# Attention and a tanh-shrink MLP on one core: the last twelve attention steps take their scores in pairs, with a down product between, and two stores change queue

## The chip, the cores and the metric

One core of a Trainium2 chip runs the whole program. The metric is the device time of one execution in microseconds (us). The profiler's times count from the first instruction of the execution that was profiled.

## The reference

For each of 4 batches and 8 heads (768 tokens, 64 dims), queries and keys are assigned to one of 16 clusters; a query attends only to keys of its own cluster. The attention output feeds an MLP with the activation h - tanh(h).

```python
q_assign = np.argmax(np.einsum('bhsd,hcd->bhsc', q_n, c_n), axis=-1)
k_assign = np.argmax(np.einsum('bhsd,hcd->bhsc', k_n, c_n), axis=-1)
mask = q_assign[:, :, :, None] == k_assign[:, :, None, :]
scores = np.where(mask, scale * (q @ k.transpose(0, 1, 3, 2)), -1e9)
attn = softmax(scores);  x = attn @ v          # (4, 8, 768, 64) -> (3072, 512)
h = x @ w_in                                    # w_in 512 x 2048
out = (h - np.tanh(h)) @ w_out                  # w_out 2048 x 512
```

## The kernel before

The attention runs as 96 **steps** (`steps`): per batch four pairs of heads, per pair two halves of the queries, per half three steps of two key chunks each. A step on TensorE is one score group (`sc`, line 544, eight matmuls in the trace: 64 rows of the array for each of two heads), then on ScalarE the exponential (line 566), on VectorE the **select** (line 576, four instructions: weight kept where the cluster codes agree), on GpSimd the running sum of the weights (`sum`, lines 588 and 592), and on TensorE the value product (`av`, line 601). The scores lie in two PSUM buffers, one for each key chunk; a group can start on a buffer when the select has read it.

The MLP of the batch before fills the time between. It is done by Strassen's scheme: **up products** (`pu`) and, for each of seven factor products and each block of 128 tokens, a **down product** (`pd`, line 1301: 32 matmuls in the trace, 16 in the program, each in two passes) whose result VectorE adds to running sums (`w_in`, `c`, line 1317). The list `fill` holds these items with weights, and each step takes as many as its share of the weight (`spent`, `whole`). Items and the other work of a step (`todo`) are written out by hand, so each engine runs exactly the order that the program lists.

TensorE works in two forms here: the scores use 64 rows by 128 columns (a trace row shows `64*128`), av, pu and pd use 128 rows by 64 columns (`128*64`). A product can also be written in the scores' form (`rows_`, `three_in_rows`): then a down product needs two of the three PSUM buffers `ps_f` and each result is added in two instructions. `runs(at)` names the steps at which the scores of the next three steps are issued together with such products between; the last twelve steps (84 to 95) are not among them: there each step has one score group, one av and mostly one pd.

Around it: `check_done` and `check_on` read inputs again (`again`, two buffers): `check_done` reduces two loaded tiles on VectorE (lines 1776 and 1781), `check_on` issues two new loads on SyncE's queue (SP). For the row sums, SP carries `list`, `each`, `back` and `den` through DRAM: VectorE's reciprocal of `each` (line 714), then the store `back` (line 716), then four loads `den` (line 737). `set_aside` stores factors of one block, and a sum of them that VectorE makes in `u` (line 1266), for later. `divide` takes reciprocals of `den` in three parts (line 764), and GpSimd adds them up (`inverses`, line 768). After step 95 the rest is the tail: `pu` of the last batch and then its down products (`pp`).

Of the kernel before, what the change touches and what calls it, by code (L numbers as in the profile page):

```python
# [58 lines left out]
def kernel(  # L59
# [120 lines left out]
    def fast():  # L180
# [677 lines left out]
        behind = []  # L858
# [346 lines left out]
        def strassen_items(b: int):  # L1205
# [33 lines left out]
            def weight(i: int):  # L1239

                return 4.55 if aside_ else 3.4
# [10 lines left out]

            def set_aside(which: int):

                d = [i for i in range(len(ASIDE)) if ASIDE[i][0] == b]
                for i in d:
# [12 lines left out]
                    behind.append(lambda total_=total_, i=i: nc.sync.dma_start(  # L1269
# [8 lines left out]
            def down_product(k_: int, j: int, between, rows_=False):  # L1278
# [66 lines left out]
                if j < 2:  # L1345
                    if k_ == 2:
                        behind.append(lambda: lower_aside(6, j))
                    elif k_ == 4:
                        behind.append(lambda: lower_aside(3, j))
                    if (k_, j) in SET_ASIDE:  # L1350
                        behind.append(lambda: set_aside(SET_ASIDE[k_, j]))
# [142 lines left out]
            def group(at: int):  # L1494
# [64 lines left out]
                if final:  # L1559
                    add(m, m, u0)  # L1560
                    nc.sync.dma_start(row(0, 1, 0)[:, 0:HC], quarters[:, 0])
                    nc.sync.dma_start(row(0, 1, 1)[:, HC:HM], quarters[:, 3])
# [284 lines left out]
        def runs(at: int):  # L1847

            return 4 * HALF < at < 7 * HALF - 1 and at % NS == NS - 1 and at % (2 * HALF) < 2 * HALF - 1

        fill, whole, spent, since, over = [], 0.0, 0.0, 0, 1
        for at, (n, half, s) in enumerate(steps):
# [21 lines left out]
            if run:  # L1874
                coming = now + fill
                for _ in range(NS - 1):
# [5 lines left out]
                while len(now) < first_ones + 1:  # L1882
# [3 lines left out]
            elif runs(at + 1):  # L1886
                ups_left = sum(len(it) == 4 for it in fill)
                if ups_left < 3 * (NS - 1):
# [17 lines left out]
            if run:  # L1906
                take(n, half)
                if half == 1 and joined(n):
                    total_both(n)
# [17 lines left out]
                begin(steps[at + NS])  # L1927
                while off:
                    off.pop(0)()
                begun |= set(steps[at + 1 : at + NS + 1])  # L1930
                selected |= set(steps[at + 1 : at + NS + 1])
                held = [
                    lambda i=i, to=steps[at + NS]: select(*to[:2], 2 * to[2] + i) for i in range(2)
# [67 lines left out]
            if following and not run:  # L2001

                if half == 1 and s == NS - 1 and joined(n):
                    todo.insert(len(todo) - 1, lambda n=n: total_both(n))
# [9 lines left out]
            if not run and not runs(at + 1):  # L2014
                todo += behind
                behind.clear()
# [28 lines left out]
            if "raw" in late_pools:  # L2045
                if not run and not runs(at + 1) and at != 7 * HALF:
# [46 lines left out]
        for it in late + behind:  # L2093
# [240 lines left out]
```

## Time and profile before

| | us |
|---|---|
| three runs | 925.0, 922.12, 924.77 (median 924.77) |
| the profiled execution, its own time | 922.68 |
| its span, first to last instruction | 920.8 |

The mean granted TensorE clock over the span is 0.999 of full speed. Steps 84 to 95 lie between 653 us (score group of step 84) and 751 us; the tail's first up product that needs new differences (`diff`) starts at 759.88 us, and the last stage (`pp`) at 829.6 us.

### The profile page before, as it was taken

The page shows a single profiled execution, that of the slowest core. Times are in us where ns is not written, and L with a number is a line of the kernel's source. Part 1 is how long each engine was busy: PE and PEld are TensorE (multiplying, and loading weights), DVE is VectorE, ACT ScalarE, POOL GpSimd, SP SyncE. Part 2 cuts the span into 40 slices and gives each one's busy share as a digit, 9 for nine tenths or more (in the row PEclk, how much of TensorE's full clock was granted, in tenths as well). Part 3 has the DMA queues.
Part 4 walks back from the last instruction along what each step waited for, and adds up shares of the span by engine and source line. Part 5 has one row for each costly group of instructions (what it writes and reads, how often), then busy time and mean ns, then how long its engine had stood idle before and what let it go on. Part 6 is the DMA issues. An engine that isn't in the chain of part 4 may idle for free.

```text
span 920.8 us, 18740 instructions
## 1 busy us (share of the span) xinstructions
PE 908.1 (99%) x7286; PEld 498.5 (54%) x7286; DVE 692.9 (75%) x1280; ACT 295.2 (32%) x466; POOL 523.6 (57%) x403
## 2 busy tenths in 40 slices
PE   8999999999999999999999999999999999999997
PEld 4434433356653454445666664555455554449997
DVE  7779777887799598667477477767697587867995
ACT  5676653234333233333321121343231311221000
POOL 0236433467878565977765565787776866772000
PEclk9999999999999999999999999999999999999999
DMA  8777583794428985375584746566546745524532
GB/s 168 226 221 180 155 194 105 229 266 141 107 86 224 272 261 141 120 189 175 159 191 151 186 143 169 177 179 161 178 150 205 230 156 155 189 103 151 196 105 85
DMA packets 187439, 158.37 MB, mean 172 GB/s; under 512 B 119200, under 2 KB 161744, under 8 KB 184144
## 3 DMA queue, kind: packets, MB, share of 16 engines
q1 hardware_dynamic: 177696, 134.40, 51.9%
q0 software_dynamic: 6048, 20.98, 6.9%
q10 hardware_dynamic: 3600, 1.74, 0.7%
q8 instruction: 59, 0.97, 0.4%
q14 instruction: 36, 0.29, 0.1%
HBM read 130.33 MB, written 26.75 MB: 171 GB/s over the span
## 4 chain that ended last, share of the span: by engine, by line
PE 92%; DVE 4%; ACT 1%; issue 1%; DMA 1%; POOL 0%; SPq 0%; DVEq 0%; ACTq 0%
PE pu L1021 20%; PE sc L544 15%; PE av L601 14%; PE pd L1301 12%; PE pp L1519 9%; PE o L803 6%; PE pu L1012 5%; PE h L787 5%; PE hd L1152 3%; PE sim L405 1%; DVE e L576 1%; PE den L674 1%; PE den L647 1%; PE den L627 1%; POOL G L1215 0%
## 5 line engine op out<-in xcount | busy, mean ns | idle before, releaser
L592 POOL TENSOR_TENSOR sum<-sum,e 128x768 f32<-128x768 f32 x112 | 206.5, 1844 | 78.7 <-DVE e L576 73.9
L576 DVE SCALAR_TENSOR_TENSOR e<-row,code,sc 128x384 f32<-128x384 bf16 x336 | 184.0, 608 | 56.7 <-ACT sc L566 31.6
L566 ACT ACTIVATE sc<-sc 128x768 f32<-128x768 f32 x168 | 126.4, 793 | 203.0 <-PE sc L544 182.4
L544 PE MATMUL sc<-t,t 64*128 64x384 f32 x768 | 149.1, 505 | 1.6 <-DVE e L576 1.1
L601 PE MATMUL av<-e,vals 128*64 128x384 f32 x768 | 143.4, 495 | 0.0
L1021 PE MATMUL pu<-xT,w_in 128*64 128x384 f32 (+1 forms) x872 | 132.5, 441 | 0.2 <-DVE c L1317 0.2
L1215 POOL TENSOR_TENSOR G<-G,th 128x768 f32<-128x768 f32 (+1 forms) x51 | 88.1, 1745 | 58.1 <-ACT th L1213 58.0
L1301 PE MATMUL pd<-w_in,G 128*64 128x256 f32 (+1 forms) x960 | 108.8, 379 | 0.0
L544 PEld LDWEIGHTS sc<-t,t 64*128 64x128 f32 x768 | 67.8, 186 | 70.5 <-issue 32.7
L1021 PEld LDWEIGHTS pu<-xT,w_in 128*64 128x64 f32 x872 | 61.6, 137 | 62.2 <-issue 50.2
L1301 PEld LDWEIGHTS pd<-w_in,G 128*64 128x64 f32 (+1 forms) x960 | 74.0, 147 | 35.6 <-issue 6.3
L601 PEld LDWEIGHTS av<-e,vals 128*64 128x64 f32 x768 | 49.7, 136 | 77.3 <-issue 73.5
L588 POOL TENSOR_TENSOR sum<-e 128x768 f32<-128x768 f32 x28 | 52.4, 1872 | 60.4 <-DVE e L576 46.4
L1021 PE MATMUL pu<-diff,w_in 128*64 128x384 f32 x416 | 74.1, 488 | 0.5 <-DVE u L1006 0.4
L1213 ACT ACTIVATE th<-G 128x768 f32<-128x768 f32 (+1 forms) x51 | 39.5, 806 | 107.8 <-DVE G L1006 90.9
L803 PE MATMUL o<-w_out,g 128*64 128x512 f32 x256 | 57.4, 593 | 0.0
L1021 PEld LDWEIGHTS pu<-diff,w_in 128*64 128x64 f32 x416 | 29.3, 137 | 37.9 <-issue 31.5
L1006 DVE TENSOR_TENSOR G<-pu,u 128x384 f32<-128x384 f32 x72 | 38.8, 550 | 13.5 <-PE pu L1021 12.1
L1012 PE MATMUL pu<-diff,w_in 64*128 64x384 f32 x160 | 45.8, 482 | 0.0
L1012 PE MATMUL pu<-xT,w_in 64*128 64x384 f32 x152 | 45.1, 482 | 0.0
L787 PE MATMUL h<-xT,w_in 128*64 128x384 f32 x256 | 42.8, 486 | 0.0
L638 ACT COPY xT<-av 128x384 f32<-128x384 f32 x32 | 15.3, 480 | 82.1 <-PE av L601 82.0
(283 smaller groups left out, 1286.0 us busy)
## 6 DMA issues: line engine op xcount, KB each, us to landing
w_in<-up_factors SPq DMA_DIRECT2D x32, 896.0 KB
w_in<-down_factors SPq DMA_DIRECT2D x25, 1024.0 KB
again<-in_moe_w_in_dram SPq DMA_DIRECT2D x32, 256.0 KB
again<-in_moe_w_out_dram SPq DMA_DIRECT2D x32, 256.0 KB
vals<-in_v_dram SPq DMA_DIRECT2D x32, 192.0 KB
raw<-in_moe_w_in_dram POOLq DMA_DIRECT2D x12, 512.0 KB, 4.8
row<-q_codes SPq DMA_DIRECT2D x29, 192.0 KB
raw<-in_moe_w_out_dram POOLq DMA_DIRECT2D x10, 512.0 KB, 4.8
```

The costliest lines, as they stand in the source:

```text
L544: nc.tensor.matmul(sc[i][:, h, 0:TB], lhsT=turned[n, 1][r].rearrange("p a n -> p (a n)")[:, j * P : (j + 1) * P], rhs=turned[n, 0][r, half ...
L566: nc.scalar.activation(out=out, in_=sc[i][:, :, 0:TB], func=ACT.Exp, scale=SCALE)
L576: nc.vector.scalar_tensor_tensor(out=e[:, h].rearrange("p (j n) -> p j n", n=P), in0=rows[n, half][:, h], scalar=(codes[n][:, h, 1, j : j ...
L592: nc.gpsimd.tensor_tensor(out=s, in0=s, in1=pair[i], op=ALU.add)
L601: nc.tensor.matmul(avs[n, half][h * D : h * D + D], lhsT=vals[n][:, h, j], rhs=e[i][:, h], start=(j == 0), stop=(j == NCH - 1),)
L787: nc.tensor.matmul(h[r], lhsT=w_in[i][:, c, o * P : (o + 1) * P][:, r], rhs=xT[c][:, half], start=(c == 0), stop=(c == CD - 1),)
L803: nc.tensor.matmul(acc[sub][r], lhsT=gs[f % HF][:, f // HF, sub * P : (sub + 1) * P][:, r], rhs=w_out[f // FQ][:, f % FQ], start=(f == seq ...
L1012: return nc.tensor.matmul(ps, lhsT=streams[base + i][r, c, k_], rhs=right[c][r], start=start, stop=stop)
L1021: nc.tensor.matmul(ps[r], lhsT=streams[base + i][:, c, k_, r], rhs=right[c], start=(c == 0), stop=(c == CH - 1),)
L1215: nc.gpsimd.tensor_tensor(out=t, in0=t, in1=th, op=ALU.subtract)
L1301: nc.tensor.matmul(out_, lhsT=w, rhs=x, start=(i == 0), stop=(i == HF - 1))
L1519: nc.tensor.matmul(ps[r], lhsT=left[:, i, r], rhs=right[i], start=(i == 0), stop=(i == HQ - 1),)
```

## The change

The steps 84 to 95 get runs of two: `runs` returns 2 at the steps 83, 85, ..., 93. At such a step the program issues the score group of the next step, the selects of it, one chunk of the filling work in the scores' form (three up products at step 83, one down product after), and the score group of the step after that. The weights of the down products of batch 2 become 5.4 for the first twelve and 3.3 for the last two (4.55 for all before). `check_done` and `check_on` now also stand in a step ahead of a run of two, and in the run itself ahead of its selects. The stores of the sums set aside get a list of their own, `stores`. The two first of the four last stores go to ScalarE's queue, where the other two are.

```diff
--- before.py
+++ after.py
@@ -855,7 +855,7 @@
         SET_ASIDE = {
             (0, 0): 1, (0, 1): 5, (1, 0): 2, (1, 1): 4, (2, 0): 7, (3, 0): 6, (5, 0): 3
         }
-        behind = []
+        behind, stores = [], []
         aside = dram.tile([len(ASIDE), 7, P, HF + HQ, P], F32, name="aside", bufs=1)
 
         def up_maker(q: int):
@@ -1238,7 +1238,10 @@
 
             def weight(i: int):
 
-                return 4.55 if aside_ else 3.4
+                if not aside_:
+                    return 3.4
+                i = i // HCH * (HCH - aside_) + i % HCH
+                return 5.4 if i < 12 else 3.3
 
             def lower(j: int, which: int, part: int):
 
@@ -1250,8 +1253,13 @@
                 else:
                     nc.gpsimd.tensor_tensor(out=a12, in0=a12, in1=a11, op=ALU.subtract)
 
+            def store_sums():
+                while stores:
+                    stores.pop(0)()
+
             def set_aside(which: int):
 
+                store_sums()
                 d = [i for i in range(len(ASIDE)) if ASIDE[i][0] == b]
                 for i in d:
                     c = slice(ASIDE[i][1] * P, (ASIDE[i][1] + 1) * P)
@@ -1266,7 +1274,7 @@
                     nc.vector.tensor_tensor(
                         out=total_, in0=t[:, 0:HQ], in1=t[:, HQ:HF], op=ALU.add
                     )
-                    behind.append(lambda total_=total_, i=i: nc.sync.dma_start(
+                    stores.append(lambda total_=total_, i=i: nc.sync.dma_start(
                         aside[i, SLOT[which], :, HF : HF + HQ], total_
                     ))
 
@@ -1342,7 +1350,7 @@
                     lower(j, 6, 1)
                 elif which in (7, 4):
                     lower(j, 3, k_ - 3)
-                if j < 2:
+                if aside_ and j < 2:
                     if k_ == 2:
                         behind.append(lambda: lower_aside(6, j))
                     elif k_ == 4:
@@ -1558,8 +1566,8 @@
                 )
                 if final:
                     add(m, m, u0)
-                    nc.sync.dma_start(row(0, 1, 0)[:, 0:HC], quarters[:, 0])
-                    nc.sync.dma_start(row(0, 1, 1)[:, HC:HM], quarters[:, 3])
+                    nc.scalar.dma_start(row(0, 1, 0)[:, 0:HC], quarters[:, 0])
+                    nc.scalar.dma_start(row(0, 1, 1)[:, HC:HM], quarters[:, 3])
                 yield
                 pair = bank()
                 if final:
@@ -1846,7 +1854,9 @@
 
         def runs(at: int):
 
-            return 4 * HALF < at < 7 * HALF - 1 and at % NS == NS - 1 and at % (2 * HALF) < 2 * HALF - 1
+            if at >= 7 * HALF - 1:
+                return 2 * (at % 2 and at < 8 * HALF - 1)
+            return NS * (at > 4 * HALF and at % NS == NS - 1 and at % (2 * HALF) < 2 * HALF - 1)
 
         fill, whole, spent, since, over = [], 0.0, 0.0, 0, 1
         for at, (n, half, s) in enumerate(steps):
@@ -1873,19 +1883,19 @@
             run, chunks = runs(at), []
             if run:
                 coming = now + fill
-                for _ in range(NS - 1):
+                for _ in range(run - 1):
                     size = 1 if coming[0][1] == 2 else 3
                     assert all(len(it) == 4 for it in coming[:size]) or size == 1
                     chunks.append(coming[:size])
                     coming = coming[size:]
                 first_ones = sum(len(it) for it in chunks)
-                while len(now) < first_ones + 1:
+                while len(now) < first_ones + (run == NS):
                     now.append(fill.pop(0))
                     spent += now[-1][0]
                 now = now[first_ones:]
             elif runs(at + 1):
                 ups_left = sum(len(it) == 4 for it in fill)
-                if ups_left < 3 * (NS - 1):
+                if ups_left < 3 * (runs(at + 1) - 1):
                     for _ in range(ups_left % 3):
                         now.append(fill.pop(0))
                         spent += now[-1][0]
@@ -1904,9 +1914,10 @@
                     if not masked(*to[:2]):
                         spread(*to[:2])
             if run:
-                take(n, half)
-                if half == 1 and joined(n):
-                    total_both(n)
+                if s == NS - 1:
+                    take(n, half)
+                    if half == 1 and joined(n) and run == NS:
+                        total_both(n)
                 for i, it in enumerate(chunks):
                     to = steps[at + 1 + i]
                     begin(to)
@@ -1924,13 +1935,13 @@
                     else:
                         it[0][2](lambda: None, True)
                     putting[0] = False
-                begin(steps[at + NS])
+                begin(steps[at + run])
                 while off:
                     off.pop(0)()
-                begun |= set(steps[at + 1 : at + NS + 1])
-                selected |= set(steps[at + 1 : at + NS + 1])
+                begun |= set(steps[at + 1 : at + run + 1])
+                selected |= set(steps[at + 1 : at + run + 1])
                 held = [
-                    lambda i=i, to=steps[at + NS]: select(*to[:2], 2 * to[2] + i) for i in range(2)
+                    lambda i=i, to=steps[at + run]: select(*to[:2], 2 * to[2] + i) for i in range(2)
                 ]
             elif following and at >= NS - 1 and following not in begun:
                 begin(following)
@@ -1998,10 +2009,10 @@
             if following and following not in selected:
                 todo += [lambda i=i, to=following: select(*to[:2], 2 * to[2] + i) for i in range(2)]
                 selected.add(following)
-            if following and not run:
+            if following and run < NS:
 
                 if half == 1 and s == NS - 1 and joined(n):
-                    todo.insert(len(todo) - 1, lambda n=n: total_both(n))
+                    todo.insert(max(len(todo) - 1, 0), lambda n=n: total_both(n))
             if LOAD in stages:
                 stages[LOAD]()
             if TURN_Q in stages:
@@ -2011,9 +2022,9 @@
             todo += route_items if isinstance(route_items, list) else [route_items]
             todo += late
             late = []
-            if not run and not runs(at + 1):
-                todo += behind
-                behind.clear()
+            if at >= 7 * HALF:
+                todo += stores + behind[:1]
+                del stores[:], behind[:1]
             if divides:
                 if not taken:
                     todo.append(lambda n=n, half=half: total(n, half))
@@ -2043,7 +2054,7 @@
             if at in EXTRAS_AT:
                 todo.append(lambda e=EXTRAS_AT.index(at): fetch_extra(e))
             if "raw" in late_pools:
-                if not run and not runs(at + 1) and at != 7 * HALF:
+                if not run and runs(at + 1) < NS and at != 7 * HALF:
                     todo += [check_done, check_done, check_on, check_on]
                 if p == HP - 1 and half == 1 and s == NS - 2:
                     todo += [lambda b=b, c=c: right_factors(b, c) for c in range(CH - 1)]
@@ -2090,7 +2101,7 @@
             putting[0] = False
             if not now:
                 between()
-        for it in late + behind:
+        for it in late + behind + stores:
             it()
         right_factors(B - 1, CH - 1)
         tail = strassen_items(B - 1)
```

Three places of the order that the change makes, as the program has it.

TensorE in the middle of the last twelve steps; `t_` names are the queries and keys of one pair of heads, and `sim` is the assignment of the next pair. Before, steps 87 and 88:

```order
L544 MATMUL sc<-t_5265,t_5249 128x384 x4
L601 MATMUL av<-e,vals 64x384 x4
L1301 MATMUL pd<-w_in_136,G 64x256 x16
L544 MATMUL sc<-t_5265,t_5249 128x384 x4
L601 MATMUL av<-e,vals 64x384 x4
L1301 MATMUL pd<-w_in_138,G 64x256 x16
```

Now, the pair of steps 86 and 87 (a `pd` whose output reads 128x256 is in the scores' form; its line is 1309 now):

```order
L544 MATMUL sc<-t_5276,t_5258 128x384 x4
L1309 MATMUL pd<-w_in_137,G 128x256 x16
L544 MATMUL sc<-t_5276,t_5258 128x384 x4
L405 MATMUL sim<-t_5702,bd 32x192 x4
L405 MATMUL sim<-t_5690,bd 32x192 x4
L601 MATMUL av<-e,vals 64x384 x4
L1309 MATMUL pd<-w_in_136,G 64x256 x16
L601 MATMUL av<-e,vals 64x384 x4
```

Two score groups stand around one product now, and both av around the next.

VectorE and SP around the selects of step 88. `again_...` are the tiles read for a check, `largest` is what `check_done` writes, `e` what a select writes. Before, VectorE:

```order
L1266 TENSOR_TENSOR u_5969<-S1_3125 128x512
L1317 SCALAR_TENSOR_TENSOR c_5971<-pd_5941,w_in3_139 128x256
L1776 TENSOR_REDUCE largest_69<-again_5922 128x1
L1776 TENSOR_REDUCE largest_69<-again_5924 128x1
L576 SCALAR_TENSOR_TENSOR e_6017<-row_5792,code_5492,sc_5987 128x384 x2
```

Now, VectorE:

```order
L1274 TENSOR_TENSOR u_5976<-S1_3125 128x512
L1325 SCALAR_TENSOR_TENSOR c_5978<-pd_5950,w_in3_139 128x256
L1784 TENSOR_REDUCE largest_69<-again_5881 128x1
L1784 TENSOR_REDUCE largest_69<-again_5883 128x1
L1784 TENSOR_REDUCE largest_69<-again_5990 128x1
L1784 TENSOR_REDUCE largest_69<-again_5992 128x1
L576 SCALAR_TENSOR_TENSOR e_6009<-row_5820,code_5514,sc_5999 128x384 x2
```

And SP now, with the loads that the third and fourth of these reductions read:

```order
L716 DMA back2_5941<-each_70 128x12
L928 DMA w_in1_137<-down_factors_149 128x2048
L1277 DMA aside_150<-u_5938 128x512
L1270 DMA aside_150<-S1_3125 128x8x128
L737 DMA den_5813<-back2_5941 64x384 x2
L737 DMA den_5983<-back2_5941 64x384 x2
L1772 DMA again_5990<-in_k_dram 128x384
L1772 DMA again_5992<-in_k_dram 128x384
```

Two checks follow each other ahead of the selects of step 88 now, and the second one's loads stand on SP behind the loads `den`.

GpSimd at the end of the twelve steps. Before:

```order
L768 TENSOR_TENSOR inverses<-inverses,den 128x384
L1251 TENSOR_TENSOR G<-G 128x4x128
L1325 DMA out_dram<-c 128x256
L592 TENSOR_TENSOR sum<-sum,e 128x768 x2
L1325 DMA out_dram<-c 128x256
```

Now, with VectorE's order behind it, from the adds of the row-form product of steps 94 and 95 to the selects of step 95:

```order
L768 TENSOR_TENSOR inverses<-inverses,den 128x384
L1254 TENSOR_TENSOR G<-G 128x4x128
L592 TENSOR_TENSOR sum<-sum,e 128x768 x2
L1254 TENSOR_TENSOR G<-G 128x4x128
```

```order
L1325 SCALAR_TENSOR_TENSOR w_in_139<-pd,w_in_139 128x256 x2
L1325 SCALAR_TENSOR_TENSOR c<-pd,w_in_139 128x256
L1325 SCALAR_TENSOR_TENSOR c<-pd,c 128x256
L764 RECIPROCAL den<-den 128x128 x3
L767 TENSOR_TENSOR xT<-xT,den 128x384
L576 SCALAR_TENSOR_TENSOR e<-row,code,sc 128x384 x4
```

TensorE behind that, now, from the score group of step 94 to the first up product of the tail:

```order
L544 MATMUL sc<-t_5702,t_5690 128x384 x4
L1309 MATMUL pd<-w_in_138,S_3125 128x256 x16
L544 MATMUL sc<-t_5702,t_5690 128x384 x4
L601 MATMUL av<-e,vals 64x384 x4
L1309 MATMUL pd<-w_in_138,S_3125 64x256 x16
L601 MATMUL av<-e,vals 64x384 x4
L647 MATMUL den<-sum,ones 64x384 x2
L1309 MATMUL pd<-w_in_137,G 64x256 x32
L1021 MATMUL pu<-xT,w_in_136 64x384 x8
```

The row sums `den` of step 95 have two products behind them now, where they had one (the last two products of the batch, formerly one on either side). The order on GpSimd is nearly the same, but the score group of step 95 is issued one product earlier now, and the adds of that product stand ahead of the reciprocals on VectorE.

## Rows read from the trace of the kernel before

**Rows 1.** The page: busy time and share of the span of each engine.

```profile
PE 908.1 (99%) x7286; PEld 498.5 (54%) x7286; DVE 692.9 (75%) x1280; ACT 295.2 (32%) x466; POOL 523.6 (57%) x403
```

**Rows 2.** Windows, step 84 to tail: us; busy PE, PEld, DVE, ACT, POOL; clock; DMA share.

```profile
653.00:760.00 107.00, 105.36 (x788) 54.67 (x788) 76.02 (x121) 27.83 (x43) 73.57 (x54) 1.00 0.61 193
```

**Rows 3.** Timeline of TensorE, one of the last steps: start, us, line, shapes.

```profile
719.01 1.56 PE L544 MATMUL sc<-t,t 64*128 64x384 f32 x8
...
721.85 3.62 PE L1301 MATMUL pd<-w_in,G 128*64 128x256 f32 x32
725.40 1.56 PE L544 MATMUL sc<-t,t 64*128 64x384 f32 x8
```

**Rows 4.** Timeline of TensorE where an earlier run stands.

```profile
527.88 1.46 PE L544 MATMUL sc<-t,t 64*128 64x384 f32 x8
529.17 3.62 PE L1301 MATMUL pd<-w_in,S 64*128 64x256 f32 x32
532.62 1.46 PE L544 MATMUL sc<-t,t 64*128 64x384 f32 x8
534.01 3.67 PE L1301 MATMUL pd<-w_in,S 128*64 128x256 f32 x32
```

**Rows 5.** Waits of TensorE from 655 to 760 us: total, times, longest.

```profile
PE sc L544 <- DVE e L576: 1.1, 2, 0.8
```

**Rows 6.** Timeline of VectorE: a check whose loads had been issued just before.

```profile
549.76 0.42 DVE L1781 TENSOR_REDUCE smallest<-again 128x1 f32<-128x256 f32 x1 [0.33 <-DMA again<-in_moe_w_out_dram]
```

**Rows 7.** Timeline of SP: DMA issues, start and us of the issue.

```profile
546.58 0.81 SPq L1766 DMA_DIRECT2D again<-in_moe_w_out_dram  x2
...
685.48 5.99 SPq L737 DMA_DIRECT2D den<-back  x4
...
725.13 0.32 SPq L716 DMA_DIRECT2D back<-each  x1
729.06 2.40 SPq L737 DMA_DIRECT2D den<-back  x4
```

**Rows 8.** Timeline of TensorE at the assignment of the last pair.

```profile
677.07 0.86 PE L405 MATMUL sim<-t,bd 128*32 128x192 f32 x16
```

**Rows 9.** Timeline of VectorE: that assignment, a sum set aside, and the end.

```profile
677.99 0.60 DVE L415 STREAM_TRANSPOSE sim<-sim 128x384 f32<-128x384 f32 x1 [0.42 <-PE sim L405]
...
680.88 0.22 DVE L714 RECIPROCAL each<-each 128x12 f32<-128x12 f32 x1
...
685.46 0.68 DVE L1266 TENSOR_TENSOR u<-G 128x512 f32<-128x512 f32 x1
686.06 2.31 DVE L1266 TENSOR_TENSOR u<-S 128x512 f32<-128x512 f32 x1
...
739.27 0.42 DVE L1317 SCALAR_TENSOR_TENSOR c<-pd,w_in 128x256 f32<-128x256 f32 x1
739.61 2.56 DVE L764 RECIPROCAL den<-den 128x128 f32<-128x128 f32 x3
...
744.11 2.19 DVE L576 SCALAR_TENSOR_TENSOR e<-row,code,sc 128x384 f32<-128x384 bf16 x4 [0.68 <-ACT sc L566]
```

**Rows 10.** Timeline of TensorE: score group of step 95, and the row sums after it.

```profile
742.27 1.56 PE L544 MATMUL sc<-t,t 64*128 64x384 f32 x8
...
748.55 1.46 PE L601 MATMUL av<-e,vals 128*64 128x384 f32 x8
749.84 0.82 PE L647 MATMUL den<-sum,ones 128*64 128x384 f32 x4
```

**Rows 11.** Timeline of GpSimd at the same place.

```profile
742.26 1.36 POOL L768 TENSOR_TENSOR inverses<-inverses,den 128x384 f32<-128x384 f32 x1 [1.71 <-DVE den L764]
743.58 1.27 POOL L1251 TENSOR_TENSOR G<-G 128x512 f32<-128x512 f32 x1
...
745.41 4.05 POOL L592 TENSOR_TENSOR sum<-sum,e 128x768 f32<-128x768 f32 x2
```

**Rows 12.** Timeline of ScalarE's queue: the last store.

```profile
914.94 0.36 ACTq L1572 DMA_DIRECT2D out_dram<-again  x1
```

## The prediction

> **What bounds the kernel now.** I read the page's busy line first: TensorE is busy for 908.1 of the 920.8 us, VectorE for 75%, GpSimd for 57% [rows 1]. The windows then tell whether that holds where the change is made: from the score group of step 84 to the tail's first new up product TensorE works 105.36 of 107 us at a granted clock of 1.00, VectorE 76.02, GpSimd 73.57 [rows 2]. So a term of the change counts only if it shortens TensorE's own time or makes TensorE wait; the other engines have 30 us to spare, but not at every place. The waits of TensorE in that stretch are short: 1.1 us, twice, for selects [rows 5]. There is little idle time to win back, and much to lose.
>
> **TensorE's own time.** A step alone takes 6.39 us from its score group to the next (719.01 to 725.40), with two changes of form in it, into the scores' form and out [rows 3]. Its parts without a change: a score group with a row-form product behind it 1.29 (527.88 to 529.17), a product 3.45 (529.17 to 532.62) [rows 4], a value product behind a down product 1.29 (748.55 to 749.84) [rows 10]. That is 6.03, so going in and out costs 0.36. Six pairs stand for twelve single steps: **-2.2 us**. A product in the scores' form takes what it takes in the other: 721.85 to 725.40 holds a product and a change of form, 3.55 against 3.45 [rows 3, 4]. The products and their count are the same; the three up products of step 83 and the new weights only move them (0). A row-form product adds its result in two instructions: five more adds of 0.42 [rows 9] on VectorE, covered by its 31 idle us [rows 2].
>
> A rule speaks against that cover. In the run at 529.17 the next row-form score group and product follow with no gap [rows 4]. The Trainium skill, TensorEngine Tiling (Array Packing), Gotcha 1: PSUM Pressure, says that row tiles write to different PSUM banks and that software must keep them apart; by it the five second adds could each hold TensorE up, 2.1 us in all. This trace does not bear that out.
>
> **The waits that go.** In a pair the selects of the first step have a whole product ahead of the second score group, and those of the second have two value products and a product; the two waits of 1.1 us [rows 5] should go: **-1.1** (0 if they come back elsewhere).
>
> **The selects of step 88.** Here a wait comes in. VectorE has two checks in front of these selects, and the loads of the second stand on SP behind the store `back`, the loads and stores of about 1.75 MB around it, and the four loads `den`. I set a clock to 0 at the score group of step 86. TensorE: that group with one change of form 1.39 (532.62 to 534.01) [rows 4], product to 4.84, group of step 87 to 6.23, `sim` 0.79 (677.07 to 677.86 [rows 8], with the modelled overlap left out) to 7.0, value product to 8.3, product to 11.8, value product to 13.1, group of step 88 to 14.4, product to 17.9. Then the group of step 89 wants the two PSUM buffers that the selects of step 88 read.
>
> VectorE gets `sim` at 7.15 (677.07 to 677.99) [rows 8, 9]. The assignment takes 2.9 up to the reciprocal (677.99 to 680.88), a sum set aside 0.68, the reciprocal 0.22: 10.95 [rows 9]. `back` needs 3.9 from its issue to the first `den` (725.13 to 729.06): 14.9. The four `den` issues take 2.40: 17.3 [rows 7]. The loads for the check are issued then; the row of an earlier pair gives 3.2 from the first issue to the reduction that waited for it (546.58 to 549.76) [rows 6, 7]: 20.5. The last reduction, 0.42 [rows 6], ends at 20.9, and half of the four selects, 2.19 [rows 9], frees the first buffer at 22.0. Due was 17.9: TensorE waits 4.1, and 0.4 more for the second buffer, 4.5. With the longer `den` issues, 5.99 at 685.48 [rows 7], it is 8.1. I take **+5.5**: the row of 2.40 is of the same chain later in the program, but 1.75 MB are queued ahead here (1, 0.25 and 0.5 by their shapes), with a DMA share of 0.61 over the stretch [rows 2]. Queued behind these reductions on VectorE are the selects, and the score group and everything after it wait for them. To be on time the selects must start by 16.8, before the loads have even been issued.
>
> A page prices such a chain lower. The trace shows 3.9 and 3.2 us for the two transfers [rows 6, 7]. The Trainium skill, DMA: Bandwidth & Descriptors, Anatomy of one DMA, fits about 2.0 us and the bytes over 436 GB/s to a transfer (measured for those that GpSimd issues); by that estimate the wait is near 2.1 and the sum ends at 925.6. The trace's rows are longer than the page.
>
> **Small waits behind it.** A late VectorE still has sums to set aside ahead of the selects of steps 89 and 90. One took 0.68, and another right after it 2.31 [rows 9]. Two such differences are 3.3 us; each pair of score groups has nearly ten us of TensorE's products and value products between it and the next, so I put **+0.7**, from 0 to 3.3.
>
> **The row sums at the end.** A clock at 0 for the score group of step 94: product from 1.39 to 4.84, group of step 95 to 6.23, value product to 7.5, product to 11.0, value product to 12.3; then `den` (line 647) wants the sum that GpSimd makes of step 95's weights. Formerly that group's start and the sum's end lay 7.2 us apart (742.27 and 745.41 + 4.05) and `den` started at 749.84, 7.6 after the group [rows 10, 11]; now the start lies at 4.84 and `den` is due 7.5 later, so nothing may be late. But VectorE has the selects of step 94, then four adds, then the three reciprocals ahead of step 95's selects. The adds follow the row-form product: 4.84 to 6.4 at 0.34 to 0.42 each (739.27 to 739.61). The reciprocals take 2.56 [rows 9], to 9.05, where formerly they were over at 742.17, before the group began. GpSimd then adds the inverses, 1.36, and does one `lower`, 1.27 [rows 11], to 11.7, and the sum takes 3.7 to 4.05 more: 15.4 at the least. TensorE waits **+3.1** (12.3 to 15.4); from 2, if GpSimd works without VectorE beside it, to 4. The two products that used to stand on both sides of `den` now both stand behind it and cannot fill this.
>
> **The first check pair** (in front of the selects of step 84) is hidden: its loads are issued a whole step before, 3.2 us against 6.39 [rows 3, 6, 7]. The number of checks does not change.
>
> **The last stores.** All four stand on ScalarE's queue now, at 0.36 each [rows 12]: the last is issued about one issue later, **+0.3** (0 to 0.4).
>
> **The sum**: -2.2 -1.1 +5.5 +0.7 +3.1 +0.3 = +6.3. The profiled execution's own time is 922.68, which is 2.1 below the median of the three runs, so **929.0 us**. With the bounds, from -3.3 +4.5 +2 = +3.2 to -2.2 +8.1 +3.3 +4 +0.4 = +13.6, all at one end: 925.9 to 936.3.
>
> **The rivals.** *Faster*: one mechanism, VectorE's lead. Each pair issues its second score group a product earlier than a single step would, so ScalarE and VectorE have up to 3.45 us more [rows 4]. If that lead covers the selects of step 88 (started by 16.8) and the last sum (done by 12.3), only -2.2 -1.1 +0.3 is left: 919.7. For it speaks VectorE's spare time [rows 2]; against it that both are late by a chain, not by load. Chance 0.17. *The same*: the loads of the second check land before the selects of step 88 are due (an issue of `den` that doesn't wait for `back`, say), and the small waits and the row sums stay: -3.3 +0.3 +0.7 +3.1 = +0.8, 923.5. Against it is the order on SP. Chance 0.18. *SP is quick*: the four `den` issues take 0.32 each, as `back` did [rows 7], 1.3 in place of 2.40, and the wait at step 88 is 3.4: 926.9. Chance 0.12. *PSUM*: the second adds are not covered, 5 x 0.42 = 2.1 more, 931.1; the run of rows 4 has no such gap. Chance 0.05.
>
> **How the numbers follow.** The forecast itself has 0.48. A measurement here tells 0.3%, 2.8 us, from no change. Faster is the first rival, 0.17; the same is the second, and the quick end of the third, 0.22; slower the rest, 0.61. The range should leave out 2 in 10: from 921 (half to two thirds of the first rival, 0.11, lie below) to 934.5 (most of the two waits at their upper ends, 0.07, lie above). I call it 921.0 to 934.5. The forecast's own range is 925.9 to 936.3.
>
> **What would show it.** In the changed profile: score groups in twos with 4.7 us between their starts; a wait of TensorE at the score group of step 89 of 4 to 8 us, released by a select, with VectorE's check waiting for the DMA of `again` before it, and on SP the four `den` issues ahead of those loads; a wait of about 3 us at line 647 for GpSimd's sum; the last store 0.3 us later behind the last product. I am wrong if the check at step 88 doesn't wait, if another engine's wait of several us stands between 655 and 760, or if the time of a score group and a product changes in the scores' form.

## The result, and the profile after

The changed kernel takes 933.38 us (median of six, 932.73 to 934.87), the kernel before 924.71 us (median of six): a ratio of 1.0102, 95% interval 1.0088 to 1.0115. That is 8.7 us slower. The forecast had said slower, with 929.0; the time lies inside the range. But 929.0 is 4.3 us above the measured median of the kernel before, and the loss is twice that.

The page's busy line of the changed kernel; TensorE is busy for 4 us more than in [rows 1], in a span that is 12.2 us longer:

```profile
PE 912.1 (98%) x7286; PEld 507.5 (54%) x7286; DVE 695.6 (75%) x1286; ACT 295.4 (32%) x466; POOL 524.6 (56%) x403
```

The waits of TensorE in the changed kernel, the two longest. The two waits of [rows 5], 1.1 us in all, are gone:

```profile
PE sc L544 <- DVE e L576: 5.4, 1, 5.4
PE den L647 <- POOL sum L592: 3.3, 1, 3.3
```

Both forecast waits are there, each once. The first is at the score group of step 89. TensorE's timeline around it:

```profile
690.55 1.56 PE L544 MATMUL sc<-t,t 64*128 64x384 f32 x8
691.94 3.62 PE L1309 MATMUL pd<-w_in,G 64*128 64x256 f32 x32
701.00 2.93 PE L544 MATMUL sc<-t,t 64*128 64x384 f32 x8 [5.43 <-DVE e L576]
703.86 2.83 PE L601 MATMUL av<-e,vals 128*64 128x384 f32 x8
706.47 3.84 PE L1309 MATMUL pd<-w_in,G 128*64 128x256 f32 x32
710.14 1.46 PE L601 MATMUL av<-e,vals 128*64 128x384 f32 x8
```

VectorE's timeline at the same place, the reductions of the two checks and the selects of step 88:

```profile
690.56 1.00 DVE L1784 TENSOR_REDUCE largest<-again 128x1 f32<-128x384 f32 x2
698.79 1.01 DVE L1784 TENSOR_REDUCE largest<-again 128x1 f32<-128x384 f32 x2 [7.23 <-DMA again<-in_k_dram]
699.72 2.18 DVE L576 SCALAR_TENSOR_TENSOR e<-row,code,sc 128x384 f32<-128x384 bf16 x4
```

And SP's issues ahead of it:

```profile
687.70 0.33 SPq L716 DMA_DIRECT2D back<-each  x1
...
689.55 3.96 SPq L737 DMA_DIRECT2D den<-back  x4
693.55 1.15 SPq L1772 DMA_DIRECT2D again<-in_k_dram  x2
```

This is the chain of the forecast, link by link: TensorE waits for a select, the select stands behind a check, the check waits 7.23 us for loads, and the loads stand behind the four `den`.

What the forecast did not have is in the third and fourth of TensorE's rows: the score group takes 2.93 us and not 1.56 as at 690.55, the value product 2.83 and not 1.46 as at 710.14. The windows of the changed kernel give the reason (us, busy PE, PEld, DVE, ACT, POOL, then the granted clock):

```profile
700.00:701.00 1.00, 0.00 (x1) 0.03 (x1) 1.00 (x3) 0.00 (x0) 0.01 (x1) 0.54 0.00 0
...
705.00:706.00 1.00, 1.00 (x6) 0.40 (x4) 1.00 (x3) 0.00 (x0) 0.98 (x2) 0.50 0.95 284
706.00:707.00 1.00, 1.00 (x8) 0.41 (x6) 1.00 (x3) 0.00 (x0) 1.00 (x2) 0.55 1.03 280
707.00:708.00 1.00, 1.00 (x14) 0.62 (x12) 1.00 (x2) 0.00 (x0) 1.00 (x2) 1.00 0.95 227
```

TensorE stood idle from 695.56. By the shares in these slices the clock fell to 0.50 (1.2 of 2.4 GHz) at about 700.1, while TensorE was still idle, and came back at about 706.9. The Trainium skill, TensorE: Matmul & The Clock Gate, Part 1, says that the engine falls to half its clock when it has been idle; these rows agree.

The second wait is at the row sums of step 95. TensorE's timeline:

```profile
752.43 1.86 PE L601 MATMUL av<-e,vals 128*64 128x384 f32 x8
757.63 1.13 PE L647 MATMUL den<-sum,ones 128*64 128x384 f32 x4 [3.35 <-POOL sum L592]
758.54 8.55 PE L1309 MATMUL pd<-w_in,G 128*64 128x256 f32 x64
766.92 5.33 PE L1021 MATMUL pu<-xT,w_in 128*64 128x384 f32 x32
```

VectorE's reciprocals ahead of the selects, and GpSimd's sum behind the inverses and the subtraction, each from its engine's timeline; they answer to [rows 9, 11]:

```profile
748.11 2.57 DVE L764 RECIPROCAL den<-den 128x128 f32<-128x128 f32 x3
...
751.19 2.18 DVE L576 SCALAR_TENSOR_TENSOR e<-row,code,sc 128x384 f32<-128x384 bf16 x4
```

```profile
750.77 1.36 POOL L768 TENSOR_TENSOR inverses<-inverses,den 128x384 f32<-128x384 f32 x1 [1.72 <-DVE den L764]
752.09 1.28 POOL L1254 TENSOR_TENSOR G<-G 128x512 f32<-128x512 f32 x1
753.33 4.25 POOL L592 TENSOR_TENSOR sum<-sum,e 128x768 f32<-128x768 f32 x2
```

Here too the clock falls, this time when TensorE works again; the two products behind `den` take 8.4 us (758.54 to 766.92) and not 6.9:

```profile
758.00:759.00 1.00, 1.00 (x8) 0.42 (x6) 0.97 (x1) 0.20 (x1) 1.00 (x1) 0.55 0.00 0
...
760.00:761.00 1.00, 1.00 (x8) 0.56 (x6) 1.00 (x1) 0.00 (x0) 0.66 (x1) 0.50 0.97 286
761.00:762.00 1.00, 1.00 (x10) 0.57 (x8) 1.00 (x3) 0.00 (x0) 0.00 (x0) 0.74 1.00 292
```

One part of the 12.2 us is not the change's. At the score group of step 72, ahead of every edit on TensorE, the changed kernel is already 2.2 us later. The row of before, and the one of after:

```profile
547.75 1.56 PE L544 MATMUL sc<-t,t 64*128 64x384 f32 x8
```

```profile
549.97 1.56 PE L544 MATMUL sc<-t,t 64*128 64x384 f32 x8
```

The kernel before with only its stores moved (below) has this group at 549.32, and the other profiled executions lie between 548.08 and 550.40; the one of before is the earliest of all. So the stretch of the change is compared from a point ahead of it, the score group of step 77 (588.36 before, 590.58 after), to the tail's first new up product (759.88 and 772.08): 171.52 and 181.50 us, **+9.98**.

### The profile page after: what moved, and what is told of

Read it like the earlier page. It is cut to its first block, busy times and chain, and to the rows that moved or that the text cites. A ratio compares the mean times of both kernels' runs of the same rounds, so it can differ in the third digit from the quotient of the medians.

```text
span 933.0 us, 18740 instructions
## 1 busy us (share of the span) xinstructions
PE 912.1 (98%) x7286; PEld 507.5 (54%) x7286; DVE 695.6 (75%) x1286; ACT 295.4 (32%) x466; POOL 524.6 (56%) x403
## 4 chain that ended last, share of the span: by engine, by line
PE 83%; DMA 6%; DVE 5%; issue 2%; SPq 1%; POOL 1%; ACT 1%; ACTq 0%; DVEq 0%; POOLq 0%
PE pu L1021 20%; PE pd L1309 12%; PE sc L544 12%; PE av L601 11%; PE pp L1527 9%; PE pu L1012 6%; PE h L787 4%; PE hd L1152 3%; PE o L803 3%; PE sim L405 1%; DMA back<-each 1%; DVE e L576 1%; DMA hot<-q_codes 1%; DMA q_codes<-qc 1%; PE den L674 1%
## 5 line engine op out<-in xcount | busy, mean ns | idle before, releaser
L601 PE MATMUL av<-e,vals 128*64 128x384 f32 x768 | 145.4, 498 | 0.0
L1021 PE MATMUL pu<-xT,w_in 128*64 128x384 f32 (+1 forms) x864 | 130.4, 440 | 0.0
L1309 PEld LDWEIGHTS pd<-w_in,G 128*64 128x64 f32 (+1 forms) x960 | 78.1, 155 | 33.8 <-issue 7.5
L1021 PE MATMUL pu<-diff,w_in 128*64 128x384 f32 x400 | 71.5, 488 | 0.4 <-DVE u L1006 0.4
L1012 PE MATMUL pu<-diff,w_in 64*128 64x384 f32 x176 | 49.6, 482 | 0.0
L1012 PE MATMUL pu<-xT,w_in 64*128 64x384 f32 x160 | 48.5, 482 | 0.0
```

What stands on the lines that cost most here:

```text
L601: nc.tensor.matmul(avs[n, half][h * D : h * D + D], lhsT=vals[n][:, h, j], rhs=e[i][:, h], start=(j == 0), stop=(j == NCH - 1),)
L1012: return nc.tensor.matmul(ps, lhsT=streams[base + i][r, c, k_], rhs=right[c][r], start=start, stop=stop)
L1021: nc.tensor.matmul(ps[r], lhsT=streams[base + i][:, c, k_, r], rhs=right[c], start=(c == 0), stop=(c == CH - 1),)
L1309: nc.tensor.matmul(out_, lhsT=w, rhs=x, start=(i == 0), stop=(i == HF - 1))
```

## The experiments

The first four ask whether the two waits are the loss, and what the clock has to do with it. The kernel before was run beside each experiment: its median was 924.06 us for the first three and for the 24 unread matmuls, 923.74 for the even weights, 924.72 for the others. The ratios use these medians. Differences from the changed kernel are given between the medians as they stand; for the runs beside 924.06 they come out 0.65 us smaller when each kernel is compared with the kernel before beside it.

**The check one step later.**

```diff
-                    if i == 0 and at != 7 * HALF + 2:
+                    if i == 0 and at != 7 * HALF + 3:
                         check_done(), check_done(), check_on(), check_on()
```

> The changed kernel, but the check ahead of the selects of step 88 is left out there; its two reductions stand one step later, ahead of the selects of step 90. Theory (the check's late loads hold up step 88, and TensorE's clock stands at half after the wait, 700.5 to 706.5 us): both go, 5.4 us of wait and 3.0 us that half a clock cost, so 8.4 us less than the changed kernel, about 925.0 us and a ratio to before of 1.000, with a granted clock of 1.00 around step 89. Rival (VectorE is late at step 88 by its own load, the check only shows it): a wait of 2 us or more stays there, with half a clock behind it, and about 929 us.

Measured: 927.43 us, ratio 1.004 (1.0025 to 1.0056), 6.0 us less than the changed kernel. The wait at step 89 is gone, and no half clock stands there, so VectorE's own load is not what held step 88. But not all of 8.4 came back. A wait of 0.72 us stands at the score group of step 91 now, and in the profiled execution the second wait became dearer. (The late check stands ahead of the selects of step 90, which the group of step 91 waits for.) TensorE's timeline at the row sums in this kernel:

```profile
750.33 1.54 PE L647 MATMUL den<-sum,ones 128*64 128x384 f32 x4 [3.34 <-POOL sum L592]
751.66 9.27 PE L1309 MATMUL pd<-w_in,G 128*64 128x256 f32 x64
```

The wait is as long as in the changed kernel (3.34), but the row sums and the two products take 10.4 us up to the up product at 760.77, where they took 9.3. The executions of this kernel differ here: nine of the eleven had a mean granted clock of 0.994 to 0.997 (the profiled one 0.995) and took 926.01 to 931.67 us, two had 0.999 and took 924.76 and 924.95, which is what the theory said. In those two the clock seems not to have fallen behind the second wait; no trace shows them.

**The selects of step 95 ahead of the reciprocals.**

```diff
             todo = []
-            if not run:
+            if not run or at == 8 * HALF - 3:
                 todo, held = held, []
```

> The changed kernel, but the selects of step 95 stand ahead of the three reciprocals of the row sums on VectorE (and so the sum ahead of the inverses and of one subtraction on GpSimd). Theory: the wait of 3.3 us at the row sums (line 647) goes, and 1.6 us of half clock behind it: 5.0 us less than the changed kernel, 928.4 us. Rival (VectorE is full from 743 to 769.6 us, with some 2 us of gaps, and the reciprocals are now later): TensorE waits at the tail's first new differences instead, and only 2 to 3 us are won, 930.5 to 931.5 us.

Measured: 930.17 us, ratio 1.0065 (1.0051 to 1.0079), 3.2 us less than the changed kernel. The rival was right in part. The wait at the row sums went, but one of 1.56 us came to the tail's up products, which wait for a down product's add. TensorE's timeline in this kernel:

```profile
752.88 0.81 PE L647 MATMUL den<-sum,ones 128*64 128x384 f32 x4
753.52 7.08 PE L1309 MATMUL pd<-w_in,G 128*64 128x256 f32 x64
760.43 2.75 PE L1021 MATMUL pu<-xT,w_in 128*64 128x384 f32 x16
764.74 2.80 PE L1021 MATMUL pu<-xT,w_in 128*64 128x384 f32 x16 [1.56 <-DVE c L1325]
```

At the full clock the row sums and two products take 7.55 us (752.88 to 760.43). In the changed kernel they took 9.29, so half a clock cost 1.74 there, and in the kernel with the later check 2.9.

**Both.** The two edits above together.

> The changed kernel with both edits: the check one step later and the selects of step 95 ahead of the reciprocals. Theory: both waits and both stretches of half clock go, 13.4 us, 920.0 us, a ratio to before of 0.995: what is left of the change is the saving of form switches and select waits (3.3 us) and the last stores (0.3). Rival (a wait comes back at the tail's differences): 922 to 923 us, 0.998. Rival (row-form pairs save nothing): 924.7, 1.000.

Measured: 923.07 us, ratio 0.9988 (0.9979 to 0.9997). Both waits are out, and it takes 10.3 us less than the changed kernel, more than the 8.7 that had been lost. Left are 0.7 us at step 91 and 1.56 us in the tail, as in the kernels with one edit. TensorE's timeline at the first place, where the group of step 89 now follows the product at once, and up to the next pair:

```profile
689.75 1.56 PE L544 MATMUL sc<-t,t 64*128 64x384 f32 x8
691.14 3.62 PE L1309 MATMUL pd<-w_in,G 64*128 64x256 f32 x32
694.60 1.46 PE L544 MATMUL sc<-t,t 64*128 64x384 f32 x8
...
702.17 1.56 PE L544 MATMUL sc<-t,t 64*128 64x384 f32 x8
```

Against this kernel the two places can be priced from start to start. From the product of the pair of steps 88 and 89 to the next pair's group the changed kernel takes 19.59 us (691.94 to 711.53), this one 11.03 (691.14 to 702.17): 8.6 us. From the product of the pair of steps 94 and 95 that stands between the two value products, to the tail's first up product, it is 17.95 (748.97 to 766.92) and 12.30 (741.00 to 753.30): 5.6 us. Together the two places cost 14.2 us.

**TensorE busy while it waits.** Matmuls whose result nobody reads, ahead of the score group of step 89; the check stays as it was.

```diff
+                if at == 7 * HALF + 3:
+                    ps = ps_f.tile([P, 2 * P], F32, name="warm", tag="f")
+                    for _ in range(24):
+                        nc.tensor.matmul(
+                            ps, lhsT=ident,
+                            rhs=turned[n, 1].rearrange("p a n -> p (a n)")[:, 0 : 2 * P],
+                            start=True, stop=True,
+                        )
                 begin(steps[at + run])
```

> The changed kernel, with 24 matmuls of 128x256 whose result is not read between the row-form product of step 88 and the score group of step 89, some 5.2 us of TensorE's work where it waits 5.4 us. Theory (the clock falls because TensorE stands idle): the wait of VectorE's check stays what it was, but the clock stays at 1.00, the score group of step 89 takes 1.4 us and not 2.9, and 3.0 us are won: 930.4 us. Rival (the clock falls there for another reason): half a clock is still granted from about 700 to 706 us, and 933.4 us or more.

Measured: 936.65 us, ratio 1.0129 (1.0113 to 1.0145). I had taken 0.22 us for one of them, from the down products' rows; in this form they took 0.44, so 24 lasted 10.6 us, outlasted the wait and cost more than they gave. The score group behind them took 1.49 us, at a clock of 1.00. The mechanism showed, the size was wrong, so I ran it with 11.

> As the kernel with unread matmuls between the row-form product of step 88 and the score group of step 89, but 11 of them: they took 0.44 us each, so 24 were 10.6 us and outlasted the wait; 11 are 4.9 us, where TensorE waits 5.4 us. Theory (the clock falls because TensorE stands idle): clock at 1.00 from 695 to 710 us, the score group of step 89 in 1.4 us and the value product behind it in 1.3, and 3.0 us won against the changed kernel: 930.4 us. Rival (the clock falls there for another reason): half a clock is still granted behind the wait, and 933.4 us.

Measured: 931.18 us, ratio 1.0073 (1.0054 to 1.0093), 2.2 us less than the changed kernel. TensorE's timeline and one window:

```profile
693.60 5.02 PE L1941 MATMUL warm<-t,ident 128*128 128x256 f32 x22
699.22 1.97 PE L544 MATMUL sc<-t,t 64*128 64x384 f32 x8 [0.60 <-DVE e L576]
701.11 1.51 PE L601 MATMUL av<-e,vals 128*64 128x384 f32 x8
702.46 3.62 PE L1309 MATMUL pd<-w_in,G 128*64 128x256 f32 x32
705.91 1.46 PE L601 MATMUL av<-e,vals 128*64 128x384 f32 x8
```

```profile
700.00:701.00 1.00, 0.86 (x6) 0.33 (x4) 0.89 (x4) 0.78 (x1) 1.00 (x1) 1.00 0.00 0
```

The score group starts 5.62 us after the first unread matmul, where TensorE had stood idle for 5.44 us, so the wait for the check is untouched. But the clock is 1.00, and from the score group to the second value product it takes 6.69 us (699.22 to 705.91), where it took 9.14 (701.00 to 710.14). So the half clock cost 2.45 us, and idleness caused it: the same late start with TensorE busy leaves the clock alone, and so did the kernel with 24. Some of this is lost again, since in the profiled execution the products behind the second wait take longer here too (10.5 us, as in the kernel with the later check).

**The check's loads on ScalarE's queue.**

```diff
-                    nc.sync.dma_start(raw[:, 0 : NCH * D], src)
+                    eng = nc.scalar if checked >= len(asked) - 2 else nc.sync
+                    eng.dma_start(raw[:, 0 : NCH * D], src)
```

> The changed kernel, but the two loads of the check ahead of step 88 are issued by ScalarE and not by SP behind the four den loads. Their buffers come free at 691.6 us; on SP they were issued at 693.55 and the check got them at 698.8. Theory of the prediction (their place on SP behind back and den makes them late): issued at 691.6 they land at 696.8, the wait of TensorE shrinks from 5.4 to 3.4 us: 931 us. Rival (the transfers themselves are late, since all queues are crowded up to 698.4 us): they land where they did, and 933.4 us.

Measured: 932.2 us, ratio 1.0087 (1.0073 to 1.0102): 1.2 us less. The issue on ScalarE, and the two reductions on VectorE:

```profile
689.27 1.20 ACTq L1773 DMA_DIRECT2D again<-in_k_dram  x2
```

```profile
694.53 0.55 DVE L1785 TENSOR_REDUCE largest<-again 128x1 f32<-128x384 f32 x1 [4.83 <-DMA again<-in_k_dram]
695.89 0.55 DVE L1785 TENSOR_REDUCE largest<-again 128x1 f32<-128x384 f32 x1 [0.81 <-DMA again<-in_k_dram]
```

TensorE waits 3.93 us and not 5.43. The place on SP is worth 1.5 us of the wait, then, less than the 2 expected; the rest is the time of the loads, which took 5.3 and 6.6 us from the first issue (689.27 to 694.53 and 695.89) and on SP 5.2 (693.55 to 698.79). Both explanations hold a part.

**All moves on VectorE.** The kernel with both edits; the late check stands behind the selects of step 91 as well, the last down product's add goes ahead of the last sum set aside, and that sum behind the tail's differences.

```diff
-                    if i == 0 and at != 7 * HALF + 3:
+                    if i == 0 and at not in (7 * HALF + 3, 7 * HALF + 5):
...
-            if at >= 7 * HALF:
+            if at >= 7 * HALF and following:
                 todo += stores + behind[:1]
...
-                if not run and runs(at + 1) < NS and at != 7 * HALF:
+                if not run and runs(at + 1) < NS and at not in (7 * HALF, 7 * HALF + 4):
...
-        for it in late + behind + stores:
+        for it in late:
             it()
...
         tail = start_without(tail)
+        for it in behind:
+            it()
+        while stores:
+            stores.pop(0)()
```

> The kernel with both edits (check later, selects of step 95 first), with three more moves on VectorE: the late check once more later, behind the selects of step 91; the last down product's add ahead of the last sum set aside; and that sum behind the tail's differences. Theory: the two waits left in the kernel with both edits (0.7 us at the score group of step 91, 1.6 us at the second up product of the tail) go, 923.07 - 2.3 = 920.8 us, a ratio to before of 0.996. Rival: VectorE's chain up to the differences holds TensorE up one product later, and 922 to 923 us.

Measured: 921.55 us, ratio 0.9965 (0.9951 to 0.9979): 3.2 us faster than the kernel before, the best version here. The profiled execution, 923.34 us, is the longest of its seven. What is left, from TensorE's timeline:

```profile
760.29 1.51 PE L1021 MATMUL pu<-diff,w_in 128*64 128x384 f32 x8 [0.74 <-DVE G L1006]
```

From step 77 (591.01) to this row it is 169.28 us against 171.52 before, so 2.24 less with 0.74 of wait in it.

**The weights.** The last kernel with even weights.

```diff
-                return 5.4 if i < 12 else 3.3
+                return 4.55
```

> The kernel with all five moves on VectorE's order (921.55 us), but with the weight 4.55 for all down products of batch 2, as before the change. Prediction's term (the weights only move products and cost nothing): the same time within 1 us, 920.5 to 922.5, ratio to before 0.9965. Rival (the weights are part of what makes the pairs fit: with even ones the products stand elsewhere and TensorE waits): over 924 us, with a new wait of TensorE of 2 us or more between 490 and 770 us.

Measured: 925.07 us, ratio 1.0016 (1.0003 to 1.0029): 3.5 us more than the last kernel, and 4.5 more when each is compared with the kernel before beside it. The rival is nearer the truth, though no single wait of 2 us shows. The up products around step 83 stand elsewhere, and the second score group of the first pair waits:

```profile
662.16 1.97 PE L544 MATMUL sc<-t,t 64*128 64x384 f32 x8 [1.43 <-DVE e L576]
```

From start to start, against the kernel with 921.55, this group comes 1.6 us later behind the up products ahead of it and takes 0.5 us longer, the value product ahead of the next pair takes 0.7 us longer (2.07 against 1.39), and in the tail an up product waits 0.69 us where it waited 0.16. Together that is 3.3 of the 3.35 us by which the stretch from step 77 is longer (172.63 against 169.28).

**The stores alone.** The kernel before, with the two stores on ScalarE's queue.

```diff
-                    nc.sync.dma_start(row(0, 1, 0)[:, 0:HC], quarters[:, 0])
-                    nc.sync.dma_start(row(0, 1, 1)[:, HC:HM], quarters[:, 3])
+                    nc.scalar.dma_start(row(0, 1, 0)[:, 0:HC], quarters[:, 0])
+                    nc.scalar.dma_start(row(0, 1, 1)[:, HC:HM], quarters[:, 3])
```

> The kernel before, with only the two of the four last stores moved to ScalarE's queue. Prediction: 0.3 us more, the last of four issues of 0.36 us in a row, which 0.3% cannot tell from no change: a ratio between 0.999 and 1.002, and the last issue about 0.3 us later behind the last matmul. Rival: ScalarE's queue delays the end by more than an issue (over 1 us).

Measured: 924.31 us, ratio 0.9992 (0.9979 to 1.0004): no difference. The last issue starts 1.97 us behind the start of the last matmul group (917.00 and 915.03) and not 1.44 (914.94 and 913.50), so it is 0.5 us later; the total does not show it.

## Why the prediction came out as it did

**Right, with their places and lengths.** The two waits: 5.5 and 3.1 were forecast, 5.43 and 3.35 came. That the first length came out so close is in part luck, since its links were off in both directions. `den` was issued 2.2 us sooner than worked out and its issues took longer, 3.96 and not 2.40, so the check's loads were issued 16.75 us after the score group of step 86, for 17.3; they then took 5.2 us and not 3.2, with 1.75 MB ahead of them; and TensorE came to the score group 0.9 us later than reckoned. The 1 us that was added for the crowded queues made the sum right. The estimate that the forecast worked out from the Trainium skill (DMA: Bandwidth & Descriptors, Anatomy of one DMA), a wait of about 2.1 us, is far below the 5.43 that the trace shows.

**Right: what the change gives.** The form switches were put at -2.2 and the select waits at -1.1. With the two waits and the smaller ones behind them moved away, the best version's stretch is 2.24 us shorter than before, 2.98 without its last 0.74 us of wait. A pair without waits takes 12.42 us from score group to score group in the kernel with both edits (689.75 to 702.17), two single steps 12.78 [rows 3]. So the faster rival, 3.0 us less than before, was about the gain that is there to have (3.2 measured); VectorE's lead did not bring it, it needed the two places put in order. The second adds of the row-form products cost nothing: behind the product at 691.94 the next group waits for the check alone, and in the kernels without that check it follows at once.

**The small waits.** Put at 0.7. In the changed kernel the value product of step 87 goes on until the score group at 690.55 that follows it, some 0.5 us longer than others, since its weights come from selects that stand behind the assignment. The value product of step 95 (752.43) takes 1.86 us where it takes 1.46 with its selects first: 0.4 more, ahead of the second wait.

**Wrong: the cost of a wait.** The step that failed is the sum over the two waits, which counted them at their own length, 5.5 + 3.1 = 8.6. From start to start the two places cost 14.2 us. Each left TensorE idle and the clock fell, and the half clock cost 2.45 us behind the first and 1.74 behind the second: 4.2 us that no term held, and up to 2.9 at the second place in other kernels. The rest, some 1.2 us, is mostly time in which a group or a value product is already under way and still waits for a select: 0.5 us at the group of step 89 (it takes 1.89 us to the next row in the kernel with 11 unread matmuls, 1.38 in the kernel with both edits) and the 0.4 us of the value product of step 95. I had read the granted clock as 1.00 [rows 2] and carried it over to a kernel with waits of 3 and 5 us in it.

**Wrong: the base.** 6.3 us were added to one execution of 922.68, which is 2.0 us below the measured median; it was ahead of every other profiled execution, by 0.3 to 2.7 us, before the change begins. On the measured median the sum says 931.0; with the clock 935.2, for 933.4 measured. Part of that last difference is that the 4.2 us come from the profiled execution, the longest of the six (934.87), with a clock of 0.992 where the others have 0.994: the others lost less to it, how much less no trace shows. In the stretch itself the idle time and the clock are 5.43 + 2.45 + 3.35 + 1.74 = 12.97, less the measured 9.98 a gain of 3.0; by the 14.2 from start to start the gain is 4.2. The terms for it were -2.2, -1.1 and +0.7. Counted from start to start, the waits for selects that went are 1.9 us and not 1.1, and 0.8 us went at the tail's first up products (753.94 to 759.88 before, 766.92 to 772.08 now), against the 0.5 us that came at step 87.

**Wrong: the weights.** They were put at 0, as moving work only. With even weights the best version loses 3.5 to 4.5 us, so there the new weights are part of the gain. In the changed kernel itself they were not tried, nor was the list `stores` by itself.

## What to carry to other kernels

Where TensorE is busy nearly all the time, price a new wait of some us at its length and then look at what runs right behind it, since that may run at half the clock; here it added 45 to 52% to a wait, and up to 87% in two other kernels. When an order is tightened so that a group starts a product earlier, move the work that stood ahead of its consumers with it: two reductions and three reciprocals, ahead of the selects that TensorE waits for, turned a gain of 3 us into a loss of 9. And add a forecast to the median of the runs, after seeing how far the profiled execution stands from it.

## What the runs showed of the hardware

The same wait of 3.3 us at the row sums had different prices: half a clock cost 1.74 us in the changed kernel and 2.9 in two others (the later check, the 11 unread matmuls), where the clock stood at 0.50 for some 3.4 and 6.8 us. A longer wait was not dearer: in the kernel with 24 unread matmuls it was 3.81 us there, and the half clock again cost 1.74. Waits of 0.72 and 1.56 us in the kernel with both edits left the clock at 1.00. In the changed kernel the clock fell only after TensorE had begun to work again (0.55 in the slice at 758), in the kernel with the later check while it was still idle (0.64 in the slice at 749, where the row sums start at 750.33). The clock also differs between executions of one kernel: its mean is 0.999 in two of the eleven with the later check, and 0.998 or 0.999 in four of the six with 11 unread matmuls, as in the profiled execution before the change (0.999). What decides this was not tried. Two loads of 192 KB took 5.2 to 6.6 us in a stretch where the DMA engines' busy share stood at 0.9 to 1.2, on either engine's queue, against 3.2 us for a pair of loads of 256 KB in [rows 6, 7], in a stretch with shares of 0 to 1.0.
